# Where a split matrix is kept: token-matrix spectra divided by GpSimd early on, and half of the inverse's matrix held in SBUF

## The chip, the cores and the metric

The kernel runs on one core of a Trainium2 chip. The metric is device time in microseconds (us); the median of three runs is 2339.69 us (2337.44 to 2342.76). The engines are named as in the profile: PE is TensorE (matrix multiplication; PEld its weight loads), DVE is VectorE, ACT is ScalarE, POOL is GpSimd, SP is SyncE. Here SP issues the loads and ACT, besides its own arithmetic, issues most of the stores, so a store waits its turn in ACT's queue, and ACT's next instruction waits behind a store that is not yet allowed to start. POOL issues no transfers in this kernel.

## The reference

The input x has 8 sequences of 3008 rows and 256 channels. The reference takes a real Fourier transform along the rows, mixes the channels with a complex 256x256 matrix, soft-thresholds, transforms back, and then applies a token mixing and a channel mixing:

```python
X = np.fft.rfft(x, axis=1); Xr, Xi = X.real, X.imag
Yr = Xr @ w_r - Xi @ w_i + b_r
Yi = Xr @ w_i + Xi @ w_r + b_i
Yr = np.sign(Yr) * np.maximum(np.abs(Yr) - 0.01, 0)      # Yi likewise
x = np.fft.irfft(Yr + 1j * Yi, n=3008, axis=1)
h = np.maximum(x.transpose(0, 2, 1) @ w_tok1, 0) @ w_tok2
u = x + h.transpose(0, 2, 1)
return u + np.maximum(u @ w_ch1, 0) @ w_ch2              # w_ch1: 256 x 1536
```

The kernel computes in fp32. Where it uses PE's faster fp32r form it writes each matrix as a high and a low part and multiplies three times (high by high, high by low, low by high: `mm3`). Making the two parts is called a split: one engine copies the high part into an fp32r tile, another subtracts it from the source.

## The kernel before, in words

**Spectra.** 3008 is 47 times 64, so a transform is a 47-point step over row groups (`dft47`, 13 groups `g`, through DRAM tensor `a_d`) and a 64-point step per pair of frequencies. There are 24 frequencies of the 47-point step, taken two at a time: `kp` runs from 0 to 11. For each `kp` and batch element `forward` transforms, `mix` multiplies by the channel matrices and thresholds (result `y`, split into high and low), `inverse` multiplies `y` by the matrix `e` of that `kp` and stores the result in DRAM tensor `b_d`, and `tokens` adds `y` times the spectrum of w_tok1, called `w`, into an accumulator (PSUM tile `gp`). At the end of a unit `close` turns the accumulator into `gh` and `gl`.

**Units.** The 8 sequences make 5 units: unit 0 and unit 1 have one sequence, units 2 to 4 have two. Unit 0 runs in plain fp32 in `begin`, in which all weights are also read from 64-bit words and narrowed to fp32 (`narrow`: two ACT and six DVE instructions a piece). Units 1 to 4 run in `spectral(u)`, which is dealt out in small steps between the steps of the channel mixing (`channel`: matmuls named `ph` and `po`). From about 930 us on only the channel mixing is left (`channel7`), which the change does not touch.

**The matrices at issue.** `w` of one `kp` is a 128x512 fp32 tile (256 KB), `e` of one `kp` 128x256 (128 KB); their second halves of columns belong to the imaginary part. In `begin`, `make_w` (line 356) makes `w`: PE multiplies into `pw`, ACT scales it into `wf` (L364), ACT issues the store to DRAM tensor `w_d` (L365), and the plain `tokens` uses `wf`. `load_e` loads `e` for the plain `inverse`. In unit 1 both are loaded again (`w_d`, `in_e`), split (`split_w`: ACT, then POOL; `split_e`: ACT, then DVE; both at L156 and L159), used, and stored split by `keep_split` (L386) into `ws_d` (512 KB for each `kp`) and `es_d` (256 KB). Units 2 to 4 load those two (`load_split`, L392). The split `w` is in tile `wt`, of which there are two buffers; `bt`, the staging tile of `b_d`, has two.

**Order.** The text above is the program's order; a scheduler then fixes, ahead of time, one order of instructions for each engine, and each engine runs its own queue in that order. SP's queue and ACT's are in order too: a transfer whose wait isn't met holds back everything behind it.

## Time and profile before

| what | value |
|---|---|
| median of three runs | 2339.69 us |
| the profiled execution | 2345.68 us, its span 2343.9 us (1.8 us lie around the span) |
| PE busy | 2284.2 us, 97% of the span |
| DVE, ACT, POOL busy | 73%, 63%, 59% |
| channel mixing alone | from about 930 us to the end |

The profiled execution is 6 us above the median. "PEclk" or "clk" is the share of full TensorE clock that was granted (1.00 is 2.4 GHz, half of it 1.2 GHz). A row of the timeline shows the start, the duration of the row's instructions, the engine, the line, and in square brackets how long the engine had been idle before and what ended that.

### The profile page before, as it was taken

The page shows a single profiled execution, that of the slowest core. Times are in us where ns is not written, and L with a number is a line of the kernel's source. Part 1 is how long each engine was busy: PE and PEld are TensorE (multiplying, and loading weights), DVE is VectorE, ACT ScalarE, POOL GpSimd, SP SyncE. Part 2 cuts the span into 40 slices and gives each one's busy share as a digit, 9 for nine tenths or more (in the row PEclk, how much of TensorE's full clock was granted, in tenths as well). Part 3 has the DMA queues.
Part 4 walks back from the last instruction along what each step waited for, and adds up shares of the span by engine and source line. Part 5 has one row for each costly group of instructions (what it writes and reads, how often), then busy time and mean ns, then how long its engine had stood idle before and what let it go on. Part 6 is the DMA issues. An engine that isn't in the chain of part 4 may idle for free.

```text
span 2343.9 us, 34879 instructions
## 1 busy us (share of the span) xinstructions
PE 2284.2 (97%) x12092; PEld 1979.5 (84%) x12092; DVE 1718.1 (73%) x2788; ACT 1478.5 (63%) x2700; POOL 1371.7 (59%) x1112
## 2 busy tenths in 40 slices
PE   8999988999999999999999999999999999999998
PEld 7778878899888998888888888898888889888876
DVE  7976775766766767677677777777777777777777
ACT  6764544554554444677677677666777766767776
POOL 0001542432442330688788788778788877878885
PEclk9999999999999999999999999999999999999999
DMA  8876775766666444122212112222210222222100
GB/s 218 248 253 178 238 236 194 225 188 205 204 217 216 151 147 152 46 80 69 63 56 69 50 58 81 69 64 78 70 60 24 82 68 83 61 69 63 50 9 37
DMA packets 149806, 277.23 MB, mean 118 GB/s; under 512 B 10949, under 2 KB 94749, under 8 KB 149629
## 3 DMA queue, kind: packets, MB, share of 16 engines
q1 hardware_dynamic: 115241, 208.40, 29.3%
q10 hardware_dynamic: 34388, 66.60, 8.7%
q8 instruction: 96, 1.57, 0.3%
q14 instruction: 81, 0.66, 0.1%
HBM read 177.57 MB, written 97.39 MB: 117 GB/s over the span
## 4 chain that ended last, share of the span: by engine, by line
PE 66%; DVE 6%; ACT 1%; issue 1%; POOL 0%; DMA 0%; DVEq 0%; ACTq 0%; POOLq 0%
PE l L132 14%; PE sx L132 13%; PE sz L132 10%; PE sy L132 10%; PE sw L132 7%; PE px L492 1%; DVE ts L1128 1%; DVE ub L158 1%; PE pm L208 1%; PE pm L207 1%; PE pm L206 1%; PE gp L207 1%; PE gp L208 1%; PE gp L206 1%; DVE uf L1125 0%
## 5 line engine op out<-in xcount | busy, mean ns | idle before, releaser
L1125 POOL TENSOR_TENSOR op<-ts,op 128x512 fp32r<-128x512 f32 (+2 forms) x503 | 639.1, 1295 | 280.3 <-ACT op L1158 276.6
L1158 ACT ACTIVATE op<-ts 128x512 fp32r<-128x512 f32 (+2 forms) x504 | 311.3, 619 | 65.5 <-DVE ts L1128 50.5
L1125 DVE TENSOR_TENSOR uf<-sy,uf 128x512 f32<-128x512 f32 (+2 forms) x232 | 156.0, 672 | 222.4 <-PE sy L132 221.9
L132 PE MATMUL l<-op,ws 128*128 128x512 f32 (+2 forms) x1134 | 314.3, 385 | 0.0
L132 PEld LDWEIGHTS l<-op,ws 128*128 128x128 f32 x1134 | 212.9, 188 | 40.2
L1154 ACT ACTIVATE x<-sx 128x512 f32<-128x512 f32 (+2 forms) x252 | 148.7, 590 | 138.7 <-PE sx L132 138.2
L132 PE MATMUL sx<-ub,w 128*128 128x512 f32 (+2 forms) x756 | 211.4, 388 | 3.2 <-DVE ts L1128 2.4
L132 PE MATMUL sx<-ub,ws 128*128 128x512 f32 (+2 forms) x756 | 210.5, 387 | 2.9 <-ACT x L1154 2.9
L159 POOL TENSOR_TENSOR xtl<-xs,xth 128x256 fp32r<-128x256 f32 x84 | 73.1, 870 | 198.5 <-ACT xth L156 174.3
L159 POOL TENSOR_TENSOR yl<-z,yh 128x512 fp32r<-128x512 f32 x72 | 95.1, 1321 | 155.2 <-ACT yh L156 147.6
L132 PEld LDWEIGHTS sx<-ub,w 128*128 128x128 f32 x756 | 141.1, 188 | 34.0 <-DVE ts L1128 5.5
L132 PEld LDWEIGHTS sx<-ub,ws 128*128 128x128 f32 x756 | 142.3, 188 | 30.4 <-ACT x L1154 3.3
L1125 POOL TENSOR_TENSOR op<-b,op 128x512 fp32r<-128x512 f32 (+2 forms) x126 | 161.0, 1278 | 0.5 <-PE sy L132 0.2
L1125 DVE TENSOR_TENSOR x<-sw,x 128x512 f32<-128x512 f32 (+2 forms) x126 | 85.7, 680 | 92.1 <-PE sw L132 92.0
L206 PE MATMUL pm<-wmh,xth 128*128 128x256 f32 x504 | 147.1, 292 | 4.9 <-ACT xth L156 3.5
L208 PE MATMUL pm<-wmh,xtl 128*128 128x256 f32 x504 | 144.6, 287 | 5.8 <-POOL xtl L159 5.8
L1178 ACT ACTIVATE x<-x 128x512 f32<-128x512 f32 (+2 forms) x126 | 78.6, 624 | 108.7 <-DVE x L1125 108.7
L132 PE MATMUL sy<-op,w2h 128*128 128x512 f32 (+2 forms) x464 | 142.0, 387 | 1.4 <-DVE uf L1125 1.4
L207 PE MATMUL pm<-wml,xth 128*128 128x256 f32 x504 | 143.2, 284 | 0.0
L159 POOL TENSOR_TENSOR wt<-aw,wt 128x512 fp32r<-128x512 f32 x12 | 17.7, 1478 | 181.7 <-ACT wt L156 181.7
L132 PE MATMUL l<-op,w2h 128*128 128x512 f32 (+2 forms) x334 | 110.0, 410 | 0.0
L132 PE MATMUL sw<-ub,ws 128*128 128x512 f32 (+2 forms) x378 | 107.6, 393 | 1.7 <-DVE op L1128 1.1
...
## 6 DMA issues: line engine op xcount, KB each, us to landing
...
a<-a_d SPq DMA_DIRECT2D x36, 512.0 KB, 4.5
wt<-ws_d SPq DMA_DIRECT2D x36, 512.0 KB, 4.2
b_d<-bt ACTq DMA_DIRECT2D x36, 512.0 KB, 5.4
...
```

Of the source, the lines that this page charges most:

```text
L132: return lambda *args, **kw: self.tc.keep_in_program_order(op(*args, **kw))
L158: hi_eng.tensor_copy(out=hi, in_=src)
L159: lo_eng.tensor_tensor(out=lo, in0=src, in1=hi.bitcast(F32), op=ALU.subtract)
L206: PE.matmul(out, lhsT=wh, rhs=xh, start=start, stop=False, skip_group_check=more)
L207: PE.matmul(out, lhsT=wh, rhs=xl, start=False, stop=False, skip_group_check=more)
L208: PE.matmul(out, lhsT=wl, rhs=xh, start=False, stop=stop, skip_group_check=more)
L492: PE.matmul(pt[:, o:o + 128], lhsT=x, rhs=f2cols(2 * kp + ab), start=True, stop=True)
L1125: eng.tensor_tensor(out=out, in0=in0, in1=in1, op=op)
L1128: V.scalar_tensor_tensor(out=out, in0=in0, scalar=0.0, in1=in1, op0=MAX, op1=op)
L1154: pins[key] = S.activation(out=t, in_=src, func=func)
L1158: pins[k] = S.activation(out=ops[k][:, 0], in_=v[k] if src is None else src, func=AF.Copy if k[0] == "t" else AF.Relu)
L1178: pins["x2r"] = S.activation(out=v["x2"], in_=v["x2"], func=AF.Relu)
```

## The change

In `begin`, `make_w` no longer stores `wf`: POOL makes the split tile from it (a copy and a subtraction), and ACT stores that to `ws_d`, one `kp` later (`keep_w`). Unit 1 then loads `w` split, as the later units do. Of `e` only the first half of the columns is loaded in unit 1, in two transfers, split by ACT and DVE, and kept in SBUF (tile `es`) for all units; the second half is the first times +1 or -1 for each partition (`sgn`, two more columns of the constant `scale`), and POOL makes it anew for every `kp` of every unit (`signed_e`, tile `e1`). `w_d`, `es_d`, `split_w`, `split_e` and `keep_split` go. In `begin` the tiles of `load_w`, `load_e` and the last two `wf` are slices of `few`, which has the place that `es` takes later; the tile `sd` of unit 0 rotates through four buffers in place of eight.

```diff
@@ sum_diff, unit 0 @@
-        sd = t4([120, 2, w], "sd") if pool is None else wk.tile([120, 2, w], F32, tag=("xtl", "xf", "wt", "et")[g % 4], name="sd", bufs=2)
+        sd = t4([120, 2, w], "sd") if pool is None else wk.tile([120, 2, w], F32, tag=("xtl", "wt")[g % 2], name="sd", bufs=2)
...
@@ make_w, and what follows it @@
-        wf = pool.tile([128, 2, DT], F32, name="wf", bufs=4) if kp < KP - 2 else wk.tile([128, 2, DT], F32, tag="xtl", name="wf", bufs=2)
+        wf = pool.tile([128, 2, DT], F32, name="wf", bufs=4) if kp < KP - 2 else wc["few"][:, 8 + 2 * (kp % 2):10 + 2 * (kp % 2)]
         for i in range(2):
             S.mul(wf[:, i], pt[:, i], sc[:, 2 * min(kp, 1) + i:2 * min(kp, 1) + i + 1])
-        PUT.dma_start(out=w_d[kp], in_=wf)
+        wt = wk.tile([128, 2, 2, DT], F32R, name="wt")
+        G.tensor_copy(out=wt[:, 0], in_=wf)
+        G.tensor_tensor(out=wt[:, 1], in0=wf, in1=wt[:, 0].bitcast(F32), op=ALU.subtract)
+        keep_w(kp - 1)
+        wc["kept"] = wt
         return wf
+    def keep_w(kp):
+        if kp >= 0:
+            PUT.dma_start(out=ws_d[kp], in_=wc.pop("kept").rearrange("p a i j -> p (a i j)").bitcast(F32))
...
-    def split_w(wf, eng):
...
-    def split_e(ef, eng):
...
-    def keep_split(kp, wt, et):
...
+    def load_half_e(h):
+        ef = ld([128, KP // 2, 128], "ef")
+        DMA.dma_start(out=ef, in_=io["e"][h * KP // 2:(h + 1) * KP // 2].rearrange("k p j -> p k j")[:, :, :128])
+        return ef
+    def split_half_e(h, ef):
+        ks = slice(h * KP // 2, (h + 1) * KP // 2)
+        split(wc["es"][:, ks, 0], wc["es"][:, ks, 1], ef, S, V)
+    def signed_e(kp):
+        e1 = wk.tile([128, 2, 128], F32R, name="e1")
+        G.tensor_scalar(out=e1, in0=wc["es"][:, kp].bitcast(F32), scalar1=sgn[:, min(kp, 1):min(kp, 1) + 1], scalar2=None, op0=ALU.mult)
+        return wc["es"][:, kp], e1
     def load_split(kp):
         wt = wk.tile([128, 2, 2, DT], F32R, name="wt")
-        et = wk.tile([128, 2, 2, 128], F32R, name="et")
-        for kept, t in ((es_d, et), (ws_d, wt)):
-            DMA.dma_start(out=t.rearrange("p a i j -> p (a i j)").bitcast(F32), in_=kept[kp])
-        return wt, et
+        DMA.dma_start(out=wt.rearrange("p a i j -> p (a i j)").bitcast(F32), in_=ws_d[kp])
+        return wt
...
@@ spectral @@
+        sts = {kp: load_split(kp) for kp in range(2)}
...
+            if u == 1 and n < 4:
+                if n < 2:
+                    halves.append(load_half_e(n))
+                else:
+                    split_half_e(n - 2, halves[n - 2])
+            m = n - lag + 1
+            if 0 <= m < len(steps) and steps[m][1] == nb - 1:
+                es[steps[m][0]] = signed_e(steps[m][0])
...
-                p.inverse(kp, sts[kp][1], ys[kp])
+                p.inverse(kp, es.pop(kp), ys[kp])
...
-                sts[kp] = split_w(wf, G), split_e(ef, V)
-                if kp + 2 < KP:
-                    ws[kp + 2] = load_w(w_d, kp + 2), load_e(kp + 2)
```

The scheduler's order moves at three places. The first is ACT's queue at the end of `begin`, where the last `wf` are scaled (in the change the last two `wf` are slices of `few`). `xh` is the high part of a row group of unit 1, `a` its 47-point step. Before:

```order
L364 ACTIVATE wf_1245<-pw_1240,sc_80 128x256 [waits PE_49]
L364 ACTIVATE wf_1245<-pw_1240,sc_80 128x256
L156 CAST wt_2278<-aw_2007 128x512 [waits DMAHW1_49]
L365 DMA w_d_89<-wf_1245 128x512 [waits DMAHW5_49,Activation_49]
L156 CAST et_2281<-ef_2009 128x256
```

With the change:

```order
L365 DMA ws_d_92<-wt_1225 128x1024 [waits DMAHW7_49,Pool_49]
L355 ACTIVATE few_100<-pw_1259,sc_79 128x256 [waits PE_49]
L355 ACTIVATE few_100<-pw_1259,sc_79 128x256
L365 DMA ws_d_92<-wt_1251 128x1024 [waits DMAHW1_49,Pool_49]
L156 CAST xh_1286<-sd_1280 120x512
L365 DMA ws_d_92<-wt_1266 128x1024 [waits DMAHW2_49,Pool_49]
L156 CAST xh_1295<-sd_1283 120x512
L275 COPY a_1299<-p1_1300 120x512 [waits PE_49]
L579 ACTIVATE gh_1314<-gp_986 128x256
```

Each store now waits for POOL, and the last three stand among and ahead of the splits for unit 1 (xh) and the first instruction of `close` (gh).

The second is SP's queue at the same time: `aw` is the unsplit `w`, `wt` the split one, `b2` a load for the first chunk of channels, `raw<-in_moe_w_ch2` a piece of w_ch2. Before:

```order
L856 DMA wt2_d_88<-wt2_1174 512x1x470 [waits DMAHW5_49,DVE_49]
L353 DMA aw_1199<-a_w_87 128x512 [waits DMAHW7_49,DMAHW0_49,PE_49]
L353 DMA aw_2007<-w_d_89 128x512 [waits DMAHW2_49,DMAHW1_49,PE_49]
L189 DMA raw_1400<-in_moe_w_ch2 128x1024 [waits DMAHW3_49,DVE_49]
L189 DMA raw_1411<-in_wt2 128x940 [waits DMAHW4_49,DVE_49]
```

With the change:

```order
L856 DMA wt2_d_84<-wt2_1173 512x1x470 [waits DVE_49]
L870 DMA b2_1274<-b_d0_87 96x5x256 [waits DMAHW0_49,DMAHW3_49,DVE_49,DMAHW4_49,PE_49,Pool_49]
L388 DMA wt_2016<-ws_d_92 128x1024 [waits DMAHW6_49,DMAHW3_49,DMAHW7_49,DMAHW1_49,Pool_49]
L189 DMA raw_1409<-in_moe_w_ch2 128x1024 [waits DMAHW4_49,DVE_49]
L189 DMA raw_1420<-in_wt2 128x940 [waits DVE_49]
```

The piece of w_ch2 now stands behind a load into `wt`, whose two buffers are in use until the last two stores to `ws_d` have landed.

The third is POOL's queue in unit 1. Before:

```order
L259 TENSOR_TENSOR sd_2585<-x_2509 120x512 [waits DMAHW2_49,DVE_49,Pool_49]
L159 TENSOR_TENSOR xtl_2481<-xs_2479,xth_2480 128x256 [waits Activation_49]
L159 TENSOR_TENSOR wt_2575<-aw_2361,wt_2575 128x512 [waits DMAHW7_49,PE_49,Activation_49]
L159 TENSOR_TENSOR y_2610<-z_2631,y_2610 128x512 [waits PE_49,Activation_49]
L259 TENSOR_TENSOR sd_2701<-x_2608 120x512 [waits DMAHW6_49,DVE_49]
```

With the change:

```order
L159 TENSOR_TENSOR xtl_2467<-xs_2465,xth_2466 128x256 [waits Activation_49]
L383 TENSOR_SCALAR e1_2588<-es_2096,sc_79 128x256 [waits PE_49]
L159 TENSOR_TENSOR y_2499<-z_2520,y_2499 128x512 [waits Activation_49]
L253 TENSOR_TENSOR sd_2671<-x_2586 120x512 [waits DMAHW6_49,DVE_49]
L159 TENSOR_TENSOR xtl_2579<-xs_2577,xth_2578 128x256 [waits Activation_49]
```

A subtraction of 512 columns, which waited for ACT and for a transfer, has made way for a one-input product of 256 columns, which waits for PE.

## Rows read from the trace of the kernel before

**Rows 1.** The page: busy time of each engine, and the chain that ended last, by engine.

```profile
PE 2284.2 (97%) x12092; PEld 1979.5 (84%) x12092; DVE 1718.1 (73%) x2788; ACT 1478.5 (63%) x2700; POOL 1371.7 (59%) x1112
PE 66%; DVE 6%; ACT 1%; issue 1%; POOL 0%; DMA 0%; DVEq 0%; ACTq 0%; POOLq 0%
```

**Rows 2.** Busy time by stretches of the span. Columns: stretch; its length, and PE, PEld, DVE, ACT and POOL busy in us (instructions); granted clock, DMA share, GB/s.

```profile
100.00:150.00 50.00, 48.83 (x267) 35.24 (x268) 37.67 (x75) 32.91 (x66) 1.27 (x1) 1.00 0.87 283
150.00:225.00 75.00, 69.91 (x354) 60.88 (x354) 55.97 (x105) 39.42 (x72) 6.58 (x4) 0.95 0.65 196
...
275.00:365.00 90.00, 76.71 (x456) 67.25 (x455) 57.44 (x81) 43.10 (x85) 35.12 (x27) 0.95 0.83 266
365.00:575.00 210.00, 206.56 (x1248) 187.29 (x1247) 141.96 (x228) 104.24 (x201) 70.07 (x61) 0.99 0.63 197
575.00:750.00 175.00, 169.98 (x1080) 155.40 (x1080) 127.02 (x200) 91.77 (x179) 69.36 (x60) 1.00 0.65 202
750.00:900.00 150.00, 148.29 (x989) 138.29 (x988) 95.33 (x160) 64.82 (x134) 48.46 (x48) 1.00 0.50 168
```

**Rows 3.** The same view, two parts of unit 1's end.

```profile
331.00:338.00 7.00, 6.35 (x26) 5.51 (x25) 5.59 (x6) 2.58 (x5) 3.43 (x3) 0.53 0.47 159
...
350.00:365.00 15.00, 10.87 (x55) 9.06 (x54) 3.86 (x6) 4.54 (x10) 1.27 (x1) 0.90 0.97 340
```

**Rows 4.** The timeline of PE in unit 1's end, rows that begin after an idle time.

```profile
330.00 0.36 PE L206 MATMUL pi<-y,et 128*128 128x256 f32 x1 [1.82 <-DVE xs L502]
...
346.91 0.48 PE L206 MATMUL po<-hh,w2h 128*128 128x470 f32 x1 [1.24 <-ACT hh L936]
...
348.77 0.38 PE L208 MATMUL gp<-y,wt 128*128 128x256 f32 x1 [0.40 <-POOL wt L159]
...
352.67 0.39 PE L206 MATMUL gp<-y,wt 128*128 128x256 f32 x1 [0.95 <-ACT wt L156]
...
354.07 0.39 PE L208 MATMUL gp<-y,wt 128*128 128x256 f32 x1 [0.59 <-POOL wt L159]
...
362.47 0.76 PE L206 MATMUL po<-hh,w2h 128*128 128x470 f32 x1 [2.59 <-ACT hh L936]
```

**Rows 5.** The timeline of ACT and of its queue (ACTq, the stores) ahead of the last of those stalls.

```profile
359.33 0.59 ACT L559 COPY bt<-pi 128x512 f32<-128x512 f32 x1 [5.93 <-DMA b_d<-bt]
359.36 0.33 ACTq L386 DMA_DIRECT2D es_d<-et  x1
...
361.58 0.38 ACT L583 ACTIVATE gh<-gp 128x256 fp32r<-128x256 f32 x1 [1.66 <-DMA es_d<-et]
```

**Rows 6.** Groups by line, of POOL, ACT and DVE: line, engine, operation, out<-in, shape, count | busy us, mean ns of one | idle before.

```profile
L159 POOL TENSOR_TENSOR xtl<-xs,xth 128x256 fp32r<-128x256 f32 x84 | 73.1, 870 | 198.5 <-ACT xth L156 174.3 <-issue 12.4 <-PE gp L208 8.6
...
L159 POOL TENSOR_TENSOR wt<-aw,wt 128x512 fp32r<-128x512 f32 x12 | 17.7, 1478 | 181.7 <-ACT wt L156 181.7
...
L156 ACT CAST wt<-aw 128x512 fp32r<-128x512 f32 x12 | 7.5, 621 | 14.5 <-issue 11.7 <-DMA x<-in_x 2.7
L156 ACT CAST et<-ef 128x256 fp32r<-128x256 f32 x12 | 4.9, 405 | 0.4 <-ACT y L156 0.4
...
L159 DVE TENSOR_TENSOR et<-ef,et 128x256 fp32r<-128x256 f32 x12 | 7.0, 582 | 4.3 <-ACT et L156 4.1 <-DMA a_d<-a 0.2
```

**Rows 7.** Transfers by line: out<-in, issuing queue, count, KB each, median us from issue to landing.

```profile
b_d<-bt ACTq DMA_DIRECT2D x36, 512.0 KB, 5.4
...
ws_d<-wt ACTq DMA_DIRECT2D x12, 512.0 KB, 4.8
...
w_d<-wf ACTq DMA_DIRECT2D x12, 256.0 KB, 3.8
...
et<-es_d SPq DMA_DIRECT2D x36, 256.0 KB, 2.7
```

**Rows 8.** The timeline of PE at the end of `begin`: two `kp` of `make_w` (pw) and `tokens` (gp), and the first matmul behind `close` (pu).

```profile
125.23 1.09 PE L361 MATMUL pw<-aw,fw 128*64 128x256 f32 x8
126.25 1.99 PE L571 MATMUL gp<-held,wf 128*128 128x256 f32 x8
128.18 1.09 PE L361 MATMUL pw<-aw,fw 128*64 128x256 f32 x8
...
146.99 0.38 PE L206 MATMUL pu<-wt,gh 128*128 128x470 f32 x1
```

**Rows 9.** The timeline of ACT in `begin`: the scaling of the second `wf` (its second half), of the second-last and of the last, and the first instruction of `close`.

```profile
108.36 0.46 ACT L364 ACTIVATE wf<-pw,sc 128x256 f32<-128x256 f32 x1
...
138.16 0.84 ACT L364 ACTIVATE wf<-pw,sc 128x256 f32<-128x256 f32 x2 [1.08 <-PE pw L361]
...
142.36 0.84 ACT L364 ACTIVATE wf<-pw,sc 128x256 f32<-128x256 f32 x2
143.23 0.33 ACTq L365 DMA_DIRECT2D w_d<-wf  x1
...
145.45 0.38 ACT L583 ACTIVATE gh<-gp 128x256 fp32r<-128x256 f32 x1 [0.62 <-PE gp L571]
```

**Rows 10.** The timeline of SP and DVE there: the load of the third piece of w_ch2, and DVE's first instruction on it.

```profile
136.65 0.33 SPq L189 DMA_DIRECT2D raw<-in_moe_w_ch  x1
...
141.78 0.43 DVE L176 TENSOR_SCALAR wide<-raw 128x512 uint32<-128x512 uint32 x1 [3.70 <-DMA raw<-in_moe_w_ch]
```

**Rows 11.** The timeline of DVE and POOL in unit 1: a DVE instruction with two SBUF inputs beside a POOL instruction, and one of the same shape with POOL idle.

```profile
323.02 1.53 POOL L159 TENSOR_TENSOR wt<-aw,wt 128x512 fp32r<-128x512 f32 x1 [2.51 <-ACT wt L156]
...
323.32 1.74 DVE L180 TENSOR_TENSOR wide<-wide 128x470 f32<-128x470 f32 x1
...
327.95 0.63 DVE L180 TENSOR_TENSOR wide<-wide 128x470 f32<-128x470 f32 x1
```

More of the change, by code (lines that the diff above doesn't have):

```diff
@@ L121, in _constants @@
         "g2": g2.reshape(2, 96, TOKS).astype(f),
-        "scale": scale.transpose(1, 0, 2).reshape(128, 4).astype(f),
+        "scale": np.concatenate([scale, np.sign(scale[1::2])]).transpose(1, 0, 2).reshape(128, 6).astype(f),
     }
@@ L234, in t4 @@
         return wk.tile(shape, F32, tag="t4", name=name, bufs=2)
-    DMA.dma_start(out=f1w, in_=io["f1"])
-    split(f1r[:, 0], f1r[:, 1], f1w[:, :2], S, V)
     a_w = dram.tile([128, KH, DT], F32, name="a_w")
     wt2_d = dram.tile([128, 4, NSLOT * TOKS], F32, name="wt2_d")
-    w_d = dram.tile([KP, 128, 2, DT], F32, name="w_d")
     a_d = [dram.tile([128, KH, 512], F32, name=f"a_d{p}") for p in range(2)]
@@ L244, in tile_kernel @@
     ws_d = dram.tile([KP, 128, 2 * 2 * DT], F32, name="ws_d")
-    es_d = dram.tile([KP, 128, 2 * 2 * 128], F32, name="es_d")
     g_d = {u: dram.tile([2, 128, 2 * 2 * C], F32, name=f"g_d{u}") for u in SPILL}
@@ L345, in prepare_w1, with load_w @@
         return dft47(load, a_w, DT, 2, None, pool)
-    def load_w(src, kp):
-        if src is a_w and kp % 3 == 2:
-            aw = wc["early"].tile([128, 2, DT], F32, name="aw")
-        else:
-            aw = wk.tile([128, 2, DT], F32, tag="lw", name="aw")
-        DMA.dma_start(out=aw, in_=src[:, 2 * kp:2 * kp + 2] if src is a_w else src[kp])
+    def load_w(kp):
+        aw = wc["few"][:, 2 * (kp % 3):2 * (kp % 3) + 2]
+        DMA.dma_start(out=aw, in_=a_w[:, 2 * kp:2 * kp + 2])
         return aw
@@ L366, in make_w @@
-        return wf
+        wt = wk.tile([128, 2, 2, DT], F32R, name="wt")
[3 more added lines that the diff above has]
+        wc["kept"] = wt
+        return wf
+    def keep_w(kp):
+        if kp >= 0:
+            PUT.dma_start(out=ws_d[kp], in_=wc.pop("kept").rearrange("p a i j -> p (a i j)").bitcast(F32))
     def load_e(kp):
-        ef = wk.tile([128, 2, 128], F32, tag="le", name="ef")
+        ef = wc["few"][:, 6 + kp % 2].rearrange("p (i j) -> p i j", i=2)
@@ L370, in load_e @@
         DMA.dma_start(out=ef, in_=io["e"][kp].rearrange("p (i j) -> p i j", i=2))
         return ef
-    def split_w(wf, eng):
-        wt = wk.tile([128, 2, 2, DT], F32R, name="wt")
-        split(wt[:, 0], wt[:, 1], wf, S, eng)
-        return wt
-    def split_e(ef, eng):
-        et = wk.tile([128, 2, 2, 128], F32R, name="et")
-        split(et[:, 0], et[:, 1], ef, S, eng)
-        return et
-    def keep_split(kp, wt, et):
-        for kept, t in ((ws_d, wt), (es_d, et)):
-            PUT.dma_start(out=kept[kp], in_=t.rearrange("p a i j -> p (a i j)").bitcast(F32))
+    def load_half_e(h):
+        ef = ld([128, KP // 2, 128], "ef")
+        DMA.dma_start(out=ef, in_=io["e"][h * KP // 2:(h + 1) * KP // 2].rearrange("k p j -> p k j")[:, :, :128])
+        return ef
@@ L631, in spectral @@
         steps = [(kp, b) for kp in range(KP) for b in range(nb)]
-        a2s, ws, sts, xts, ys = {0: p.load_a(0)}, {}, {}, {}, {}
-        for kp in range(2):
-            if u == 1:
-                ws[kp] = load_w(w_d, kp), load_e(kp)
-            else:
-                sts[kp] = load_split(kp)
+        a2s, xts, ys = {0: p.load_a(0)}, {}, {}
+        sts = {kp: load_split(kp) for kp in range(2)}
+        halves, es = [], {}
         lag = 4 if nb == 1 else 3
@@ L722, in begin @@
             wc["early"] = early
+            wc["few"] = wk.tile([128, KP, 256], F32, tag="es", name="few", bufs=1)
+            f1w = early.tile([120, 3, 128], F32, name="f1")
+            wc["f1"] = f1w[:, :, :120]
+            DMA.dma_start(out=f1w, in_=io["f1"])
+            split(f1r[:, 0], f1r[:, 1], f1w[:, :2], S, V)
             wc["eye"] = early.tile([128, 128], F32, name="eye")
@@ L766, in begin @@
                 if n == NW - 1:
-                    aws.update({k: load_w(a_w, k) for k in range(3)})
+                    aws.update({k: load_w(k) for k in range(3)})
                 k = n - NW
@@ L792, in begin @@
         p.tokens(KP - 1, wfs1.pop(KP - 1), ys[KP - 1])
+        keep_w(KP - 1)
         p.close()
```

33 lines of the change are left out of this document (13 added, 20 removed).

## The prediction

> **What bounds the kernel now.** I read the busy times first: PE is busy for 2284.2 us, 97% of the span, and the chain that ended last runs over PE for 66% of it, over DVE for 6% [rows 1]. So the kernel is bound by PE, and an edit that moves no matmul can only act on what PE loses: its idle time, 2343.9 - 2284.2 = 60 us in all, and the stretches in which it runs at a lower clock. Second, the busy times by stretches show where that lies [rows 2]. Behind 365 us there is little: 3.4 us idle in 210 us, 5.0 in 175, 1.7 in 150. At the end of unit 1, from 275 to 365 us, it is 90 - 76.7 = 13.3 us, and the mean granted clock of 0.95 there is worth another 0.05 x 90 = 4.5 us: 17.8 us together. From 100 to 150 us, where the spectra of the token matrix are made, PE idles for 1.2 us only, DVE is busy for 37.7 of 50 us and the DMA engines at 0.87. So unit 1's end is where something can be won, and the stretch from 100 to 150 us is where work is added to a full house. Third, the timeline says what ended PE's waits in unit 1's end [rows 4]: twice ACT's hh (1.24 and 2.59 us), three times the split w itself (0.40, 0.95, 0.59), once DVE (1.82).
>
> **The end of unit 1.** Gone are 12 ACT copies of w at 621 ns and of e at 405 ns (7.5 + 4.9 us), 12 DVE subtractions at 582 ns (7.0 us), 12 POOL subtractions at 1478 ns (17.7 us) [rows 6]; and on the queues 12 stores of 512 KB and 12 of 256 KB, 12 loads of w of 256 KB and 12 of e of 128 KB. What comes is 12 loads of 512 KB, two loads of 384 KB with two splits of 768 columns, and 12 POOL products. The bytes fall from 14.2 MB to 7.1. The three waits for the split w, 1.94 us, go with it for certain. The wait of 2.59 us goes if ACT's queue flows: there ACT's bt waited 5.93 us for the store of an earlier bt, es_d's store stood between, and then gh waited 1.66 us more behind it [rows 5], at a DMA share of 0.97 [rows 3]. With 256 KB and 512 KB stores for each kp out of that queue, I take that wait and the other one for hh as gone (3.83 us), and the 1.82 us too, since DVE and POOL lose a subtraction each ahead of it. That is 7.6 us. The clock falls to 0.53 from 331 to 338 us [rows 3], right behind the wait of 1.82 us at 330.0 and others, so I count its 4.5 us as gone also: 12.1 us. Something will be late in their place (the chain from mix to y to inverse stays, and POOL's sd and xtl), about 1 us: I take -11. The bounds: -2, the waits for the split w alone; and -15, if the stretch becomes like that from 575 to 750 us, which idles 5.0 us in 175 and would leave 2.6 of the 17.8 here.
>
> **The beginning.** Per kp POOL now makes a copy and a subtraction of 128x512, and ACT's store grows from 256 to 512 KB and waits for POOL; there are two buffers of wt. So copy k waits for the landing of store k-2, and one turn of two kp is copy + subtraction + issue + landing. The subtraction is 1.48 us [rows 6], the issue 0.33 [rows 9]. A one-input POOL instruction of this size is not in the trace. It lies between ACT's copy of the same tile, 0.62, and the two-input subtraction, 1.48; I take the 0.87 of the 128x256 subtraction, which reads as many elements [rows 6]. The landing is 4.8 us for the same store in unit 1, with 3.8 (half the size, in this place) and 5.4 (b_d) as bounds [rows 7]. The turn is 0.87 + 1.48 + 0.33 + 4.8 = 7.48 us, 3.74 for each kp, where PE's pace is 128.18 - 125.23 = 2.95 [rows 8]. The second wf is scaled at 108.8 [rows 9], POOL has split it by 111.2, and ten kp further on it is 111.2 + 37.4 = 148.6 us. Now the queue: behind the last store on ACT stand xh, a (whose matmuls PE must have had) and gh, which before came at 145.45 [rows 9] and which pu, at 146.99 [rows 8], needs. Behind 148.6 come 0.33 for the issue and 0.62 for xh: gh at 149.6, 4 us late. With the lower bounds the turn is 6.23, no slower than PE's pace to speak of; the last wf is then ready at 143.2, split at 145.3, and gh at 146.3, 1 us late. With the upper ones it is 8.69: 111.8 + 43.5 + 0.95 = 156.2, 11 us late. PE waits there, and the one place where the trace has waits this dense lost 0.47 x 7 = 3.3 us to the clock behind them [rows 3]; I add 3.
>
> On SP's queue the first load into wt waits until store 10 has landed, some 151 us by the same working, and behind it stand a piece of w_ch2 and the rest of the next loads. That piece was issued at 136.65 and DVE had it at 141.78 [rows 10], so DVE gets it at 151 + 5.1 = 156, 14 us later. DVE is busy for 56.0 of the 75 us behind 150 [rows 2], so most of it fits; I take 1 us on PE, with 0 and 5 as bounds. The beginning in all: +4 + 3 + 1 = +8, between +1 and +19.
>
> The early part of begin costs nothing: the slices of few are as many buffers as before, and sd with four buffers in place of eight stays ahead of PE's thirteen groups. Here I go by the order of instructions, which is unchanged there; if it is wrong it is below 1 us.
>
> **Units 2 to 4.** 36 loads of 256 KB go, which landed in 2.7 us [rows 7] and for which no wait is among PE's; 36 POOL products come, 0.44 (half the copy) to 0.87 us each, 16 to 31 us on an engine that is busy for 187.9 of 535 us [rows 2]. Each waits for PE's last use of its buffer, and behind it on POOL stands y, for which PE waits; but that use lies one step back. All this runs beside PE. I take -1, between -4 and +4.
>
> **The sum** is +8 - 11 - 1 = -4 us against the profiled execution's 2345.68, so 2341.7; the median lies 6.0 us below that execution, and -4 on it gives 2335.7: 2336 us.
>
> **A rule against this change.** Where POOL and DVE meet, the rows show that they don't run side by side: L180 took 1.74 us beside a POOL subtraction that ran from 323.02 to 324.55, and 0.63 with POOL idle; 1.74 is about the 1.23 that POOL still had to run plus 0.5 [rows 11]. The Trainium skill states it in "SBUF — State Buffer", section "Who interferes with whom": VectorE instructions with two SBUF inputs or in a two-port mode share a port pair with GpSimd, and whoever comes second is blocked for the whole instruction. The trace agrees. By such a lock the beginning is dearer than my sum, and that is the second rival.
>
> **The rivals.** First: the store chain does not set the pace. A copy near 0.62 and landings near 3.8 us make it 3.1 us for each kp against 2.95, and there is slack ahead of it. For it: that landing is the one measured in this place. Against it: the DMA share there is 0.87 already, and 3.1 MB come on top. Then +1 - 12 - 1 = -12 on 2339.7: 2328. Second, on the other side: DVE's and POOL's work exclude each other between 100 and 150 us. DVE's 37.7 us [rows 2] and 12 x (0.87 + 1.48) = 28.2 us of POOL make 65.9 in 50: 15.9 us late, with 3.3 of clock behind it 19, against -12: +7, 2347. For it: rows 11, and DVE's work here is mostly of that kind. Against it: DVE would have waited for its w_ch2 piece anyway, and part of the work isn't needed for 20 us. It decides the sign as soon as the two together are more than about 12 us late. Third: unit 1's stalls are not w's. The stores of a_d and b_d and the loads for unit 2 fill the queues as before, and only the waits for w and half of the clock go: -4; with +8 and -1 it is +3, 2343. Against it speaks that half the bytes go just there. That the change doesn't do what it says I leave out: the order has 36 loads of es_d fewer and 48 products more.
>
> **How the numbers follow.** My forecast 0.40 (2336; its own range 2330 to 2341), first rival 0.20, second 0.22, third 0.18. About 0.2%, 4.7 us, is what a measurement of this kernel can tell from no change; so "faster" is below 2335.0: all of the first rival and two fifths of the forecast, 0.36. "Slower" is above 2344.4: most of the second rival and a third of the last, 0.26. The rest, 0.38, is the same. The range: the bounds of the terms give 2340 + 1 - 15 - 4 = 2322 and 2340 + 19 - 2 + 4 = 2361; I leave out the far end of the second, as all three terms would have to go wrong at once: 2323 to 2352.
>
> **What would show it.** ACT's stores to ws_d from 113 us on with a POOL subtraction as what ended the wait, one each 3.7 us, and gh near 150; the w_ch2 piece on DVE near 156; from then on PE about 8 us behind. In unit 1's stretch PE idle below 4 us and the clock near 1.00. POOL's copy of 512 columns should be near 0.87 us, its product near 0.5. I am wrong if PE reaches pu at 147 or past 156, or if unit 1 still idles above 8 us.

## The result, and the profile after

The change made the kernel slower. Its median of five runs is 2350.9 us (2347.58 to 2358.83) against 2337.86 before; the ratio is 1.0055, with a 95% interval of 1.0033 to 1.0077. Run once more among the experiments below (`after_again`) it is 1.0029 (1.0015 to 1.0044). So the median lies 13.0 us above that of before on the first occasion and some 7 us on the second. The forecast was 2336.

The profiled execution is the slowest of the five: 2358.83 us, span 2357.0, 13.1 us above the span of before. The page, first its busy times, then the chain of waits by engine:

```profile
PE 2293.6 (97%) x12092; PEld 1988.7 (84%) x12092; DVE 1720.9 (73%) x2778; ACT 1471.3 (62%) x2678; POOL 1430.3 (61%) x1172
...
PE 68%; DVE 4%; issue 1%; ACT 1%; DMA 1%; POOL 0%; DVEq 0%; ACTq 0%; POOLq 0%
```

Against [rows 1]: PE has the same 12092 matmuls and is busy 9.4 us longer, at a mean granted clock of 0.989 against 0.994, so most of the 13.1 us is slower matmuls and not idle time. By stretches, to be read against [rows 2] (the last is new; the row of before for it stands below):

```profile
100.00:150.00 50.00, 47.22 (x232) 33.06 (x233) 33.86 (x56) 26.06 (x53) 22.48 (x20) 0.93 0.74 254
150.00:225.00 75.00, 65.21 (x319) 55.94 (x319) 59.94 (x115) 39.45 (x73) 6.71 (x5) 0.91 0.63 198
275.00:365.00 90.00, 82.88 (x532) 75.19 (x531) 61.23 (x86) 42.85 (x78) 42.63 (x35) 0.96 0.72 220
365.00:575.00 210.00, 205.21 (x1226) 185.18 (x1225) 139.08 (x221) 102.75 (x198) 82.02 (x73) 0.98 0.60 185
575.00:750.00 175.00, 169.10 (x1079) 155.58 (x1078) 129.20 (x207) 91.23 (x178) 79.19 (x70) 0.99 0.58 176
750.00:900.00 150.00, 148.28 (x984) 137.55 (x982) 95.94 (x158) 65.29 (x135) 61.94 (x61) 1.00 0.41 146
900.00:925.00 25.00, 21.21 (x114) 19.71 (x114) 13.57 (x25) 7.56 (x15) 0.00 (x0) 0.93 0.57 180
```

The last stretch in before:

```profile
900.00:925.00 25.00, 24.22 (x150) 23.13 (x149) 21.69 (x41) 10.52 (x21) 0.00 (x0) 1.00 0.42 118
```

From 275 to 365 us PE gained 6.2 us of work; from 100 to 225 it lost 6.3 us of it and the clock fell; and a third place, 900 to 925, lost 3 us at a lower clock. Single instructions of PE make better marks than stretches, since all that follows is shifted. The table has the start of six of them in the timelines, in us behind those of before (101.05, 146.99, 247.7, 405.4, 892.8 and 933.4 us; the end is that of the span, 2343.9). pw is the first matmul of `make_w`, pu the first behind `close`, sx the first of `channel7`:

| kernel | first pw | first pu | first gp of unit 1 | first gp of unit 2 | last gp of unit 4 | first sx | end | ratio to before (95%) |
|---|---|---|---|---|---|---|---|---|
| change | +2.4 | +12.7 | +15.6 | +9.1 | +10.5 | +16.4 | +13.1 | 1.0055 (1.0033 to 1.0077) |
| after_again | +3.3 | +10.7 | +15.0 | +1.7 | +2.1 | +8.5 | +4.8 | 1.0029 (1.0015 to 1.0044) |
| w_only | +1.4 | +10.6 | +14.4 | +4.3 | +4.0 | +4.2 | +1.3 | 1.0014 (1.0001 to 1.0027) |
| e_only | +2.2 | +1.3 | +2.7 | +1.3 | +1.7 | +7.9 | +4.9 | 1.0036 (1.0024 to 1.0049) |
| e_swap | +3.0 | +2.1 | +7.5 | +8.9 | +8.3 | +8.3 | +5.4 | 1.0012 (0.9999 to 1.0024) |
| swap | +0.3 | +7.7 | +10.9 | -3.0 | -2.6 | -2.4 | -4.7 | 0.9996 (0.9987 to 1.0006) |
| store_sp | +2.5 | +14.8 | +18.4 | +11.9 | +10.8 | +17.2 | +13.0 | 1.0048 (1.0031 to 1.0066) |
| small_store | +1.3 | +8.8 | +17.1 | +5.8 | +4.8 | +5.0 | +1.9 | 1.0022 (1.0010 to 1.0034) |
| no_store | +1.9 | +5.8 | +13.8 | +2.9 | +2.1 | +2.1 | -2.7 | 1.0000 (0.9990 to 1.0009) |
| thin_small | +1.5 | +2.9 | +9.3 | -2.6 | -3.7 | -3.5 | -7.3 | 0.9970 (0.9955 to 0.9984) |
| pool_now | -0.4 | +9.3 | +26.9 | +14.1 | +13.3 | +13.7 | +10.3 | 1.0048 (1.0033 to 1.0063) |
| pool_high | +1.6 | +9.7 | +15.5 | +5.1 | +4.4 | +4.8 | +1.3 | 1.0004 (0.9995 to 1.0013) |
| dve_low | -1.1 | +0.5 | +12.8 | -2.5 | -3.7 | -3.5 | -6.5 | 1.0009 (0.9995 to 1.0023) |
| half_pool | +0.2 | +2.1 | +7.6 | -7.5 | -8.4 | -8.2 | -11.9 | 0.9991 (0.9980 to 1.0003) |
| swap_late | +1.4 | +8.5 | +12.6 | +1.6 | +0.2 | +0.4 | -3.0 | 1.0020 (1.0009 to 1.0032) |
| dve_low_late | +1.3 | +2.6 | +13.5 | +2.4 | +1.2 | +1.4 | -2.6 | 1.0014 (1.0003 to 1.0024) |
| half_pool_late | +0.3 | +2.5 | +9.1 | -2.2 | -2.7 | -2.5 | -6.8 | 0.9993 (0.9983 to 1.0004) |
| swap_raw | +3.2 | +10.5 | +17.3 | +9.6 | +10.0 | +10.2 | +8.0 | 1.0010 (0.9997 to 1.0023) |
| half_pool_raw | +1.6 | +4.8 | +12.3 | -3.3 | -4.0 | -3.8 | -5.0 | 0.9986 (0.9975 to 0.9997) |

The ratios leave out one execution of after_again (12940.75 us) and one of before (2809.53 us), which lie far off all others; the marks are of one profiled execution each. Executions of one kernel lie up to 15 us apart (half_pool: 2333.82 to 2348.48), so a difference of some 4 us in a mark says something only where it recurs. Two columns need care. At the first pw, where the split of w has not begun, the kernels lie from 1.1 us ahead of before to 3.3 behind, so what the split costs is read from the first pw to the first pu. Behind the first sx, where the change touches nothing, every kernel takes 1.2 to 4.8 us less than before's profiled execution did, so the column of the end favours them all by about that much.

**The beginning.** The timeline of the change, all engines:

```profile
151.15 0.72 POOL L357 CAST wt<-few 128x512 fp32r<-128x512 f32 x1 [2.55 <-DMA ws_d<-wt]
151.95 1.59 POOL L358 TENSOR_TENSOR wt<-few,wt 128x512 fp32r<-128x512 f32 x1
...
153.57 0.33 ACTq L365 DMA_DIRECT2D ws_d<-wt  x1
153.94 0.62 ACT L156 CAST xh<-sd 120x512 fp32r<-120x512 f32 x1 [4.09 <-POOL wt L358]
...
154.61 0.39 PE L206 MATMUL p<-xh,f1r 120*128 120x256 f32 x1 [2.69 <-ACT xh L156]
...
157.60 0.33 SPq L388 DMA_DIRECT2D wt<-ws_d  x1
157.82 0.39 ACT L579 ACTIVATE gh<-gp 128x256 fp32r<-128x256 f32 x1
158.02 0.41 SPq L189 DMA_DIRECT2D raw<-in_moe_w_ch  x1
...
159.66 0.59 PE L206 MATMUL pu<-wt,gh 128*128 128x470 f32 x1
...
163.56 0.43 DVE L176 TENSOR_SCALAR wide<-raw 128x512 uint32<-128x512 uint32 x1 [2.05 <-DMA raw<-in_moe_w_ch]
```

This is the picture that the prediction drew, only later: ACT's store waits for POOL, xh stands behind it for 4.09 us, PE waits 2.69 us for xh, gh comes at 157.82 (145.45 in [rows 9]), pu at 159.66 (146.99 in [rows 8]) and the w_ch2 piece at 163.56 (141.78 in [rows 10]). The same timeline 45 us earlier, POOL and DVE side by side:

```profile
107.22 1.10 DVE L179 TENSOR_TENSOR wide<-raw,wide 128x512 f32<-128x512 f32 x1
107.85 1.60 POOL L358 TENSOR_TENSOR wt<-wf,wt 128x512 fp32r<-128x512 f32 x1
108.24 1.49 DVE L504 TENSOR_TENSOR xf<-xf 128x256 f32<-128x256 f32 x1
109.65 0.68 DVE L530 TENSOR_TENSOR z<-pm,bias 128x512 f32<-128x512 f32 x1
```

The same instruction in before:

```profile
104.51 0.42 DVE L508 TENSOR_TENSOR xf<-xf 128x256 f32<-128x256 f32 x1
```

The xf of 256 columns, 0.42 us alone, lasts 1.49: it ends 0.28 us after POOL's subtraction, which ran until 109.45. Summed from 100 us to the first pu, DVE's instructions last 9.0 us longer in the change than the shortest of the same shape and operation would (8.8 in after_again, 10.1 in swap); in before it is 0.7.

**The end of unit 1** gained, as forecast. From the first gp of unit 1 to that of unit 2, PE idles for 16.2 us in before, 11.6 in the change, 9.3 in after_again and 8.8 in swap; what the clock lacks of full speed, times the length, comes to 6.8 us in before, 6.8 in the change and 1.7 in the other two. The change's profile kept two waits, one of them new:

```profile
360.32 0.38 PE L206 MATMUL gp<-y,wt 128*128 128x256 f32 x1 [2.14 <-DMA wt<-ws_d]
370.92 0.48 PE L206 MATMUL po<-hh,w2h 128*128 128x470 f32 x1 [1.59 <-ACT hh L936]
```

**The end of unit 4** is a place that the prediction doesn't speak of. `wt<-wt_d` is the load of a tile of the later stage (named wt2 in the program):

```profile
903.74 0.59 SPq L846 DMA_DIRECT2D wt<-wt_d  x1
905.79 0.34 ACTq L584 DMA_DIRECT2D g_d<-gh  x1
...
906.52 0.33 ACTq L584 DMA_DIRECT2D g_d<-gl  x1
...
914.62 1.23 DVE L1024 TENSOR_TENSOR a<-w 128x1024 f32<-128x1024 f32 x1 [4.62 <-DMA g_d<-gl]
...
922.70 0.68 PE L206 MATMUL ph<-uh,w 128*128 128x376 f32 x1 [3.79 <-ACT uf L899]
```

The view of SP's waits from 885 to 910 us (what is waited for; us in total, times, longest) names the cause of the first row:

```profile
SPq L846 <- PE gp L208: 9.9, 1, 9.9
```

Before:

```profile
880.61 0.59 SPq L846 DMA_DIRECT2D wt<-wt_d  x1
...
895.99 0.33 ACTq L588 DMA_DIRECT2D g_d<-gl  x1
```

There the load was issued at 880.61, ahead of the last gp (892.79); now it waits for the last gp, which reads the split w. It then runs beside the stores of gh and gl, DVE waits 4.62 us for gl's landing, and PE 3.79 us at the end of that chain; the granted clock was half from 921.3 us on for 6.8 us. The mark `first sx` falls 5.9 us further back there.

### The profile page after: what moved, and what is told of

It reads as the page before. It is cut to its first block, busy times and chain, and to the rows that moved or that the text cites. A ratio compares the mean times of both kernels' runs of the same rounds, so it can differ in the third digit from the quotient of the medians.

```text
span 2357.0 us, 34708 instructions
## 1 busy us (share of the span) xinstructions
PE 2293.6 (97%) x12092; PEld 1988.7 (84%) x12092; DVE 1720.9 (73%) x2778; ACT 1471.3 (62%) x2678; POOL 1430.3 (61%) x1172
## 4 chain that ended last, share of the span: by engine, by line
PE 68%; DVE 4%; issue 1%; ACT 1%; DMA 1%; POOL 0%; DVEq 0%; ACTq 0%; POOLq 0%
PE l L132 15%; PE sx L132 14%; PE sz L132 11%; PE sy L132 10%; PE sw L132 7%; PE px L488 1%; PE pm L208 1%; PE pm L207 1%; PE pm L206 1%; DVE ts L1128 1%; PE gp L208 1%; PE gp L207 1%; PE gp L206 1%; DVE ub L158 1%; PE pi L207 0%
## 5 line engine op out<-in xcount | busy, mean ns | idle before, releaser
L253 POOL TENSOR_TENSOR sd<-x 120x512 f32<-120x512 f32 x39 | 52.8, 1353 | 97.8 <-DVE xl L159 72.9
L132 PEld LDWEIGHTS sz<-g,b 96*128 96x128 f32 x836 | 106.8, 191 | 2.7
```

The lines of the kernel that those rows point to most:

```text
L132: return lambda *args, **kw: self.tc.keep_in_program_order(op(*args, **kw))
L253: eng.tensor_tensor(out=sd[:, 0], in0=x[:, 0], in1=x[:, 1], op=ALU.add)
```

## The experiments

**Halves.** `w_only` is before with the first half of the change (POOL splits in begin, unit 1 loads ws_d; e as before). `e_only` is the change with w stored unsplit, loaded into the low half of wt and split in place in unit 1:

```diff
-        wt = wk.tile([128, 2, 2, DT], F32R, name="wt")
-        G.tensor_copy(out=wt[:, 0], in_=wf)
-        G.tensor_tensor(out=wt[:, 1], in0=wf, in1=wt[:, 0].bitcast(F32), op=ALU.subtract)
-        keep_w(kp - 1)
+        PUT.dma_start(out=w_d[kp], in_=wf)
...
+        DMA.dma_start(out=wt[:, 1].bitcast(F32), in_=w_d[kp])
+        split(wt[:, 0], wt[:, 1], wt[:, 1].bitcast(F32), S, G)
```

> The change's first half alone: in begin POOL splits w and ACT stores it to ws_d, unit 1 loads it split; e, the places of the tiles and sd's eight buffers stay as before. Theory A (the beginning loses by the split of w: the chain of stores through two buffers, ACT's queue behind POOL, DVE beside POOL): pu comes at 155 to 160 us (146.99 before, 159.66 with the change), PE is 8 to 12 us behind there; unit 1's end gives back only the waits for w, 3 to 5 us; the end of unit 4, near 900 us, is as before, since the tiles lie as before. Together 3 to 9 us slower than before: 2341 to 2347. Rival B (the beginning loses by the new places: few, four buffers of sd): pu at 147 to 150, and the gain of unit 1 stands: 2332 to 2337.

> The other half alone: e resident by its first half, signs by POOL, the places of the tiles as in the change; w is stored unsplit in begin as before, and in unit 1 it is loaded into the low half of wt, split in place by ACT and POOL, and stored to ws_d. Theory A: pu at 147 to 150 us, at most the 3 us of the stretch from 25 to 50 us late; unit 1's end gives 4 to 8 us; the load of wt2 near 900 us still lies over wt and costs its 6 us: 2333 to 2342. Rival B: pu at 155 or later, as with the change, and the time is 2345 or more.

Measured: w_only reaches pu 10.6 us late and e_only 1.3 (from the first pw on, 9.2 late and 0.9 early), so the beginning loses by the split of w and not by the new places of tiles: theory A at this mark. Two expectations missed. From the first gp of unit 1 to that of unit 2, w_only gains 10.1 us, where I expected 3 to 5, and e_only 1.4, where I expected 4 to 8 (e_swap, below, even loses 1.4): the gain of unit 1 comes with w as well. That the halving of e's bytes is worth nothing is not shown by this, since e_only also splits w in place and a step later than before does. And e_only, not w_only, loses 6.2 us between the last gp of unit 4 and the first sx, though it doesn't split w in begin; with 1.0036 it came out slower than the 2333 to 2342 us that I expected.

**The place of wt.** By the addresses that the program assigns, wt2 of the later stage takes bytes 159168 to 166848 of each partition. In before, tiles that are idle by then lie there; with the change the second buffer of wt does, up to byte 160704. One line moves it 6 KB down:

```diff
-tag=("xtl", "wt")[g % 2]
+tag=("wt", "xtl")[g % 2]
```

> The change with the two tags of sd in the other order, by which wt lies 6 KB lower and no longer under the tile wt2 of the later stage. Theory A (at the end of unit 4 the load wt<-wt_d waits for the last use of wt by PE, then runs beside the store of gl, which takes 8.1 us, and the weights of the later stage come late): the load is issued at 885 to 897 us and not at 903.7, the wait of 3.79 us for uf near 922 us goes with its fall of the clock, and the time falls by 3 to 6 us: 2345 to 2348. Rival (the store of gl was slow by itself, the place has no part): the load moves but the wait and the time stay: 2349 to 2354.

> e_only with the two tags of sd in the other order. Theory A (the place of wt under wt2 costs about 6 us wherever it is so): the load wt<-wt_d near 890 us no longer waits for PE's last gp, the lag of 6 us between 900 and 925 us goes, and the time falls from 1.0036 of before to 1.0005 to 1.0020. Rival (it was chance, or comes from the signs): 1.003 or more.

> The change itself once more, beside the others on one chip, nothing edited. Theory A (of the change's 13 us some 6 are the place of wt, some 8 to 10 the beginning, some -7 to -14 the end of unit 1, the rest differs from run to run): the ratio to before is 1.002 to 1.005, the stall near 922 us is there again, and the fall of the clock at 40 us, with its 3 us, need not be. Rival (the 25 to 50 us stretch is a cost of the change): the lag of 3 us at 45 us is there again.

In swap's timeline the load goes out ahead of the last gp (890.18), and DVE's first instruction has no wait:

```profile
881.71 0.59 SPq L846 DMA_DIRECT2D wt<-wt_d  x1
...
893.38 0.33 ACTq L584 DMA_DIRECT2D g_d<-gl  x1
896.96 1.23 DVE L1024 TENSOR_TENSOR a<-w 128x1024 f32<-128x1024 f32 x1
```

Four kernels have wt under wt2 (change, after_again, e_only, store_sp): in all four the load is issued 0.42 us behind the last gp, gl's store lands in 7.4 to 7.7 us, and the way from the last gp to the first sx is 5.9 to 6.4 us longer than in before. In before, swap, e_swap and w_only the store lands in 3.2 us and the way is 0 to 0.2 us longer. Theory A, and it costs 6 us: PE idles there for 4.0 to 4.3 us in the four and 0.8 to 1.0 in the others, and only the four lose 3.4 us to a lower clock. The ratios agree: 1.0029 to 0.9996 (swap), 1.0036 to 1.0012 (e_swap). In after_again the clock falls at 23.5 us and not at 40.7, and PE is 2.3 us late at 44 us and 3.3 at 54: the rival's sign came. But swap_raw has a fall at 41.3 and is 3.2 late at the first pw, while half_pool, with the same early part as swap_raw, has no fall and is 0.2 late. So this lag comes and goes, and isn't shown to be a cost of the change.

**The beginning: who waits for whom.** `store_sp` has SP issue the stores to ws_d. `small_store` (built on swap, as all below) stores 8 columns in place of 1024 and loads wt from a_w; `thin_small` lets POOL's copy and subtraction take 8 columns of each half too; `no_store` keeps the whole split and leaves the stores out.

```diff
-            PUT.dma_start(out=ws_d[kp], in_=wc.pop("kept").rearrange("p a i j -> p (a i j)").bitcast(F32))
+            DMA.dma_start(...)                                                       # store_sp
+            PUT.dma_start(out=ws_d[kp][:, :8], in_=wc.pop("kept")[:, 0, 0, :8].bitcast(F32))   # small_store
...
+        DMA.dma_start(out=wt.rearrange("p a i j -> p (a i j)").bitcast(F32), in_=a_w[:, k:k + 4])   # k = 2 * min(kp, 10)
```

> The change with the stores to ws_d issued by SP in place of ACT; all else equal. Theory A (ACT, held up in order by stores that wait for POOL, makes the 7 us that PE loses from 145 to 158 us): ACT's xh and gh follow PE at once, pu at 152 to 154 and not at 159.66, 3 to 7 us faster than the change: 2344 to 2348. Rival (the landings through two buffers, or DVE and POOL excluding each other, set the time, whoever issues): pu at 157 or later, and SP's loads now wait for POOL too: 2350 to 2356.

> From swap (the change with wt placed lower): POOL's split of w stays whole, but each store to ws_d takes 8 columns in place of 1024, and units 1 to 4 load wt in the same size from a_w, so the tokens are multiplied by another matrix and the output is not the reference's. Theory A (the landings of 512 KB through two buffers, with ACT's queue behind them, make the beginning late): pu falls from 154.72 us in swap to 148 to 150. Rival (POOL and DVE exclude each other, the stores have no part): pu stays at 153 to 156.

> The same, and POOL's copy and subtraction take 8 of 256 columns of each half too; w is not split, the output is not the reference's. Theory A: little more is gained than in small_store, under 1.5 us at pu. Rival (POOL and DVE exclude each other): this is the step that brings pu back, from 153 to 156 in small_store to 147 to 149 here, and DVE's instructions of 128x512 from 100 to 150 us last 0.42 and 0.68 again throughout.

> From small_store: POOL's split of w whole, but no store to ws_d at all, so nothing on ACT waits for POOL any more; units 1 to 4 load wt from a_w in the same size, the tokens are multiplied by another matrix and the output is not the reference's. Theory A (what is left of the beginning's loss is ACT waiting in order for POOL's subtraction, which DVE draws out): pu falls from 155.76 us in small_store to 148 to 151, near the 149.91 of thin_small. Rival (DVE, stopped by POOL, holds PE by itself): pu stays at 153 to 156, and DVE's instructions still last up to 1.5 us.

Measured: store_sp is no better: PE waits 9.3 us at 141.86 for an aw that stands behind those stores on SP. Without the 512 KB stores pu stays where it was (+8.8 to swap's +7.7; from the first pw +7.5 to +7.4), although POOL, which waits 9.8 us in all for landings in swap, waits for none in small_store. So the landings, on which the prediction's term rests, don't set the time (2.0 us of small_store's lateness is a wait of PE for the load of an aw, which swap doesn't have; up to that much they could). Without POOL's columns it is back at +2.9 (from the first pw +1.4), and DVE's 128x512 instructions last 0.42 and 0.69 us throughout: POOL's work on w is the price. no_store lies between, at +5.8, where neither of its two theories put it; 1.9 of that lie ahead of the first pw. In the other 3.9 us PE waits 1.87 for a wf ahead of which ACT waited 2.10 for POOL, and 1.09 for one ahead of which ACT waited 2.46 for DVE. How the price divides between ACT's waits for POOL and DVE's own stops is not settled: no_store has 13.6 us of those stops, more than swap, and half of its lateness. Its timeline shows how POOL fares where DVE doesn't pause:

```profile
120.75 13.43 POOL L357 CAST wt<-wf 128x512 fp32r<-128x512 f32 x1 [2.19 <-ACT wf L355]
120.89 0.63 DVE L180 TENSOR_TENSOR wide<-wide 128x470 f32<-128x470 f32 x1
...
133.74 0.72 DVE L253 TENSOR_TENSOR sd<-x 120x256 f32<-120x256 f32 x1
134.27 1.32 POOL L358 TENSOR_TENSOR wt<-wf,wt 128x512 fp32r<-128x512 f32 x1
134.39 1.48 DVE L254 TENSOR_TENSOR sd<-x 120x256 f32<-120x256 f32 x1
```

A copy that lasts 0.61 us at its shortest lasts 13.43 here, while DVE works without a gap and nearly all its instructions keep their usual length. `pool_now` (each store issued by POOL itself, `G.dma_start`) and `pool_high` (the same, with the copy on ACT) take ACT's wait away in the real kernel:

> The change with wt placed lower (swap), and each store to ws_d issued by POOL itself right behind its subtraction, so that neither ACT nor SP waits for POOL. Theory A (ACT's wait for POOL is the price): pu at 148 to 151 us and not at 154.72, the end of unit 1 as in swap, and the time 3 to 5 us under swap: 0.997 to 0.999 of before. Rival (POOL and DVE exclude each other, whoever stores): pu at 153 or later and the time as with swap, 0.999 to 1.001; if POOL's issue of a transfer takes over 1 us, POOL is later still, and the last stores hold SP's loads of wt.

> POOL issues the stores as in pool_now, one kp later, and ACT in place of POOL makes the high part of w, so POOL works 1.3 us for each kp in place of 1.9. Theory A (ACT's wait is the price): ACT now waits for the landing of an earlier store before each copy, pu at 151 to 156. Rival (POOL and DVE exclude each other): with a third less of POOL's time pu is 1 to 3 us earlier than in pool_now.

pool_now has the same drawn-out copy (13.44 us), and the stores behind it are late with it; its rival won, and more. pool_high brings nothing at pu (8.1 us from the first pw), so the 1 to 3 us that its rival gave it didn't come.

**The same work on other engines.** `dve_low` splits w by ACT and DVE, `half_pool` by POOL's copy and DVE's subtraction:

```diff
-        G.tensor_copy(out=wt[:, 0], in_=wf)
-        G.tensor_tensor(out=wt[:, 1], in0=wf, in1=wt[:, 0].bitcast(F32), op=ALU.subtract)
+        S.copy(out=wt[:, 0], in_=wf)                                  # dve_low; half_pool keeps G.tensor_copy
+        V.tensor_tensor(out=wt[:, 1], in0=wf, in1=wt[:, 0].bitcast(F32), op=ALU.subtract)
```

> From swap: w is split in begin without POOL, the high part by ACT (12 copies of 0.62 us), the low part by DVE (12 subtractions of 0.68, 8.2 us, about what POOL's presence added to DVE: 7 us). Theory A (the price of the beginning is that DVE and POOL exclude each other, and that whoever waits for POOL waits for DVE's next pause): pu at 148 to 152 us and not 154.72, the stores to ws_d follow each other without a gap of over 5 us, and the time is 2 to 5 us under swap: 0.997 to 0.999 of before. Rival (the price is the added work in a full stretch, on whatever engine): pu at 154 or later, 0.999 to 1.003.

> From swap: POOL makes the high part (one input, 0.61 us alone), DVE the low part. Theory A: POOL's copy is still drawn out wherever DVE runs without a pause, in some places over 2 us, and DVE's subtraction waits for it in order, with all that DVE has behind it: pu at 152 to 157, no better than swap. Rival (it is the two-input subtraction on POOL that costs): pu at 148 to 152, as in dve_low.

At pu dve_low is 0.5 us late, as its theory A has it, and half_pool 2.1 (from the first pw 1.6 and 1.9), with 8.2 us more work on DVE. So it isn't the amount of work. For half_pool I had expected 152 us or later, no better than swap; its rival holds: it is the two-input subtraction on POOL that costs. The copy stays on POOL there, and lasts 1.20 us at most, since DVE's subtraction waits for it; in pool_high the copy is gone from POOL, the subtraction stays, and so does the lateness. What DVE's instructions last above their shortest goes the same way: 0.8 us in dve_low, 3.4 in half_pool, 7.2 in pool_high, 10.1 in swap. half_pool's POOL also waits 13.0 us for landings, more than swap's 9.8, which speaks once more against the landings. In the whole time little of this is left: half_pool's 0.9991, dve_low's 1.0009 and swap's 0.9996 have intervals that overlap. In dve_low, behind pu, PE waits 3.42 us for gl, which stands on DVE behind the late w_ch2 piece. Two edits, in five kernels, go after that: the loads of wt queued behind the pieces (`with tc.issue_after(...)` around the first two load_split: swap_late, dve_low_late, half_pool_late), and the third piece loaded ahead of b2 (swap_raw, half_pool_raw).

> From swap: the first two loads of the split w for unit 1 are queued on SP behind the pieces of w_ch2 and wt2, not ahead of them. Theory A (SP's queue, held by a load that waits for the last stores, brings the w_ch2 piece late to DVE, and with it gl and ul: more than the 1 us of the prediction): the piece reaches DVE at 145 to 150 us, the lag behind before at 180 us is 3 to 6 us less than in swap, the ratio 0.997 to 0.9985. Rival (1 us, as predicted): 0.999 to 1.000.

> dve_low with the same move on SP's queue. Theory A: what was left of the beginning's loss without POOL was this queue (PE's wait of 3.42 us for gl at 151.5 us, DVE standing 3.91 us at the w_ch2 piece ahead of it, and the fall of the clock from 151 to 165 us behind it): the wait and the fall go, and the lag at 180 us falls from 9.8 to 0 to 4 us; ratio 0.995 to 0.998. Rival (added work in a full stretch): the lag stays at 7 or more, ratio 0.999 to 1.002.

> half_pool with the same move. Theory A: 1 to 3 us faster than half_pool, 0.996 to 0.9985. Rival (half_pool had no loss by SP's queue): as half_pool, 0.999.

> From swap: the third piece of w_ch2 is loaded ahead of b2 on SP's queue (b2's load waits 8.2 us there for DVE), the rest as it was. Theory A (what swap loses between pu and the first gp of unit 1, 7.7 us late at the one and 10.9 at the other, is this piece, late at DVE): DVE has it before 145 us, the first gp of unit 1 is 5 to 8 us behind before, the ratio 0.997 to 0.999. Rival (DVE has no room for the piece before 150 us anyway): the first gp stays 10 to 12 us behind, ratio 0.999 to 1.001.

> half_pool with the same move. Theory A: the first gp of unit 1 is 2 to 5 us behind before and not 7.6, the ratio 0.996 to 0.9985, and this version beats both kernels. Rival: 7 to 9 us, ratio 0.9985 to 1.0005.

None of the five did what its theory A said. dve_low_late and half_pool_late came out as their rivals; swap_late (1.0020) was slower than its rival had it, and in swap_raw and half_pool_raw the first gp of unit 1 came later than theirs had it. In swap_late the load of the piece left SP at 152.73, against 153.12 in swap: ahead of it SP waits 8.8 us for DVE, and the move can't help with that. In dve_low_late, too, SP no longer waits for a store, only for DVE, yet:

```profile
152.54 0.43 DVE L176 TENSOR_SCALAR wide<-raw 128x512 uint32<-128x512 uint32 x1 [3.68 <-DMA raw<-in_moe_w_ch]
152.88 0.42 DVE L580 SCALAR_TENSOR_TENSOR gl<-gp,gh 128x256 fp32r<-128x256 f32 x1
```

With the piece early (half_pool_raw has it at DVE at 131.18) the first gp of unit 1 is still 12.3 us late. So the piece is not what costs the 1 to 18 us that the kernels lose between pu and that gp. By kind they are idle time of PE and lower clock: from pu to that gp before has 5.2 us of idle time and lacks 3.4 us by its clock, swap 5.3 and 5.3, half_pool 6.9 and 6.8, dve_low 9.2 and 11.9, pool_now 15.4 and 13.7. What starts them in each kernel stays open. half_pool_raw has the lowest ratio of all that compute the reference: 0.9986 (0.9975 to 0.9997), 0.4 to 0.7% under the change and just under before; its interval overlaps those of swap and half_pool.

## Why the prediction was wrong

**The sum's sign.** Three terms were +8, -11 and -1. By the marks of after_again they are +15 up to the first gp of unit 1, -13.3 from there to that of unit 2, +0.4 to the end of unit 4, and then +6.4 that no term stood for. swap takes away that fourth term alone, and is 0.9996 (0.9987 to 1.0006): no longer slower than before, but the forecast's -4 us (0.9983) lies outside the interval too. So two steps failed. The one that made the kernel slower is "Units 2 to 4 ... All this runs beside PE. I take -1": it counted the instructions that go and come there, and not that moved tiles change who waits for whom at the next stage's first loads. None of the rows read from before could show it.

**The beginning: mis-sized, and by the wrong mechanism.** This is the second step. The forecast +8 came from a store chain with a landing of 4.8 us. The stores to ws_d and POOL's waits for their landing are there (17.1 us in all in the change), with 3.8 us for the median landing (the lower bound) and 0.61 to 2.46 us for the copy; but shrinking the stores moved nothing at pu, and half_pool, with 13.0 us of such waits, is nearly on time. In place of +8 the change shows +15.6 and after_again +15.0 up to the first gp of unit 1: 2.4 and 3.3 ahead of the first pw, 10.3 and 7.4 from there to pu, 2.9 and 4.3 behind. In swap the three are 0.3, 7.4 and 3.2; that their sum of 10.9 is near 8 is luck, since another cause made it. The second rival, POOL and DVE excluding each other, priced at 19 with 15.9 late, named the right cause and put it too high: at pu the change is 12.7 and 10.7 late, thin_small 2.9. The Trainium skill's rule in "SBUF — State Buffer", section "Who interferes with whom", cited there, agrees with the 1.49 us of xf. The 13.43 us of the copy go beyond it: by the rule the one that comes second is blocked for one instruction of the other, and this copy lasted over 28 of DVE's. The rival's weight of 0.22 was too low, since the order put POOL's work where DVE was busy for 37.7 of 50 us [rows 2] and only few gaps were left.

**SP's queue, +1.** The w_ch2 piece came at 163.56 and not 156, because all before it was later. With the piece early, in half_pool_raw, the first gp of unit 1 came no sooner (+12.3, half_pool +7.6), so no run shows that its lateness costs PE more than the 1 us; what the queue costs by itself was not isolated, since in swap_late the piece left SP no sooner.

**The end of unit 1, -11.** Measured -6.5 in the change's profile, -13.3 in after_again, -13.9 in swap. The size is right, and so is the division in the latter two: 6.9 and 7.4 us less idle time, where the prediction had 7.6 less 1, and 5.1 less by the clock, where it had 4.5. Its source is not quite: the text gave it to the split of w and of e together, and e_only shows 1.4 of it, w_only 10.1. In the change's own profile the clock gave back nothing (6.8 us again), which with the waits of 2.14 and 1.59 us keeps it below the others; from 275 to 365 us PE idles for 7.1 us there, neither below the 4 that the prediction named nor above its 8. The third rival (the stalls aren't w's) falls.

**Early part of begin, nothing.** At the first pw the change is 2.4 us late and after_again 3.3, swap 0.3 and half_pool 0.2, whose tiles there differ from the change's only by the order of two tags, and w_only, which leaves the tiles of before, 1.4. A cost of more than 1 us is not shown, and a smaller one can't be told from this scatter.

**What would show it.** pu past 156 was named as a sign of error, and it came. POOL's product was put near 0.5 us; the group shows twice that:

```profile
L383 POOL TENSOR_SCALAR e<-es,sc 128x256 fp32r<-128x256 f32 x48 | 54.0, 1124 | 64.4 <-PE pi L208 59.8 <-DVE es L159 4.5
```

No cost of it shows: from the first gp of unit 2 to the last of unit 4 e_only is 0.4 us slower than before and e_swap 0.6 faster.
